# An own tile of 64 positions for batches 0 and 1 in the v half of a gMLP, and a new order of the program

## The chip, the cores and the metric

The kernel runs on one core of one Trainium2 chip. Its metric is the device time of one execution in microseconds (us). Of the kernel before there are three timed runs, 505.13, 502.82 and 502.2 us (median 502.82), and one profiled execution, from which all views are taken.

## The reference

There are 8 batches, 8 heads, 576 positions and 64 channels per head, so 512 model channels. The gMLP has 1024 hidden channels: 512 for u and 512 for v.

```python
# attention without a score matrix
q_s = exp(q - max(q, axis=-1));  q_s = q_s / sum(q_s, axis=-1)     # over the 64 channels
k_s = exp(k - max(k, axis=2));   k_s = k_s / sum(k_s, axis=2)      # over the 576 positions
kv  = einsum('bhsd,bhse->bhde', k_s, v)                            # 64 x 64 for each head
x   = einsum('bhsd,bhde->bhse', q_s, kv)                           # heads side by side: (8, 576, 512)
# gMLP
h    = gelu_tanh(x @ w_in)                                         # (8, 576, 1024)
u, v = h[..., :512], h[..., 512:]
v_n  = (v - mean(v)) / sqrt(var(v) + 1e-6) * g_ln                  # over the 512 channels of v
v_s  = einsum('ts,bsd->btd', w_sg, v_n) + b_sg                     # mixes the positions
out  = x + (u * v_s) @ w_out
```

Everything is float32.

## The kernel before

**Arithmetic.** A float32 operand is split into a high and a low part, both of type fp32r, and each large product is made of three matmul groups: high x high, low x high, high x low. So x is kept as `x_h` and `x_l`, v_n as `vnh` and `vnl`, the gated product as `gh` and `ulow`, the weights as `wi_h` and `wi_l` (w_in), `ws_h` and `ws_l` (w_sg), `wo_h` and `wo_l` (w_out). Making the low part of a product that stands in PSUM is a subtraction on DVE (VectorE); in some places TensorE adds minus the high part to the PSUM tile (steps named ..._neg, matmuls with `minus`), and ACT (ScalarE) then only copies.

**Steps of one batch.** q is loaded, reduced by its maximum over the channels (`q_max`, `q_sub`, `q_exp`, `q_sum`, `q_inv`, `q_mul`) and transposed. k is reduced by its maximum over the positions (`k_ma` to `k_maxb`, `k_sub`, `k_exp`), and `kv_mm` gives kv, which `kv_scale` divides by the sum of k. `x_mm` (batch 1), `xf_mm` (batch 0, in parts) or `xm_mm` (batches 2 to 7) give x transposed, channels on partitions; the steps ..._high and ..._low write `x_h` and `x_l`. `hu_mm` and `hu_part` give u, again transposed, in four pieces of 128 channels. `hv_mm` gives v with positions on partitions, tile by tile of 128 positions: x is the stationary operand, `wi_h` and `wi_l` are moved in 512 columns, 12 matmuls a tile. Per tile follow the gelu (`hv_gelu`, ACT), the statistics (`hv_stat`: bn_stats on DVE, or sums that ACT made in `hv_gelu` and `hv_sq`), `hv_pow` (POOL, that is GpSimd), `hv_norm` (DVE), `hv_high` (ACT) and `hv_low` (DVE). `sg_mm` is the product with w_sg, four pieces a batch, each with 24 matmuls over the four whole tiles and then the tail; `gate`, `gate_high` and `gate_low` follow, then `out_mm`, `out_base` (x back from its parts), `out_add` and `out_store`. The last piece of the last batch is done in two halves of the positions: `last_mm`, `last_add`, `last_store`.

**576 positions in tiles of 128.** Four tiles leave a tail of 64. The kernel before stores odd batches with the tail in front, and copies an odd batch's tail a second time, behind the 576 positions of the even batch before it. One v tile of 128 rows, `hv_mm b 4` with b even, then holds the tails of both batches (`tail`, L791; `tail_high`, `tail_low` and `tail_again` make its parts of v_n for either batch). So the v half of batch 0 is complete only when x of batch 1 stands. The second copies are the second pair in `x_places` (L720, batch 1) and `tail_places` (L703, later odd batches).

**What sets the order.** `PLAN` (L33) is a text of 1243 steps. It is run from first to last, and every engine gets its instructions in that order; nothing is reordered later. A letter at a step's end names the engine (V is DVE, A is ACT, G is POOL), where there is a choice. All instructions of DVE, ACT, POOL and of SP (the DMA queue) go through one helper (L156 in the profile), all matmuls through another (L243). PSUM has three double banks (`ps2`) and two single ones (`ps1`) which are taken in turn, so a step that writes a bank waits until the last reader of the step before it in that bank is done. Two slots each of `x_h`, `x_l`, q, k and kv are shared by the batches in turn; pieces of w_out wait in the second slots of `x_h` and `x_l` (the names `raw_x_h`, `raw_x_l`), until they are converted (`wo_a` to `wo_l`) and x of batch 1 may be written. Pieces of w_in are converted by `wi_a` to `wi_l`; `wi_x` lets TensorE do a part of it (matmuls with `ot_i,eye` and `wi_h,minus`).

## Time and profile before

| | us |
|---|---|
| three timed runs | 505.13, 502.82, 502.2 |
| profiled execution | 502.31 |
| its span | 500.2 |
| TensorE busy in the span | 484.3 |
| DVE, ACT, POOL busy | 359.8, 273.8, 149.5 |
| first product with w_in on TensorE | starts at 30.83 |
| first sg matmul of batch 0 | starts at 77.98 |

The span is the time from the first to the last instruction that the profile holds; the profiled execution's own time is 2.1 us longer. The granted clock of TensorE was 1.0. In a row of the timeline stand the start, the length, the engine, line and operation, the output and the inputs, the shapes and the number of instructions in a row of the same kind; in brackets the idle time before it and who ended it. In a row of groups stand the number of instructions, then busy time and mean in ns of one, then the idle time ahead of them and its releaser.

### The profile page before, as it was taken

What the parts mean: (1) busy time and instruction counts of PE and PEld (TensorE: products, weight loads), DVE (VectorE), ACT (ScalarE), POOL (GpSimd) and SP (SyncE); (2) the same over time, 40 slices, a digit from 0 to 9 for tenths busy, and PEclk for the clock granted to TensorE, in tenths of its full rate; (3) what the DMA queues carried; (4) which work ended last, traced back from release to release, by engine and by line L of the source; (5) the groups of instructions that cost most, each with busy time, mean ns of one, the idle gap of its engine ahead of it and who ended that gap; (6) DMA issues with size and microseconds to landing.
All of it is one profiled execution on the core that took longest, in us unless ns stands there. A gap on an engine that the chain in (4) does not pass through costs nothing.

```text
span 500.2 us, 9413 instructions
## 1 busy us (share of the span) xinstructions
PE 484.3 (97%) x3833; PEld 445.5 (89%) x3833; DVE 359.8 (72%) x634; ACT 273.8 (55%) x573; POOL 149.5 (30%) x122
## 2 busy tenths in 40 slices
...
GB/s 300 365 388 170 54 307 1 7 232 149 18 1 96 255 54 29 25 215 136 1 47 3 193 85 72 0 78 160 171 2 1 1 96 1 1 24 72 1 0 96
DMA packets 19630, 48.87 MB, mean 98 GB/s; under 512 B 1666, under 2 KB 8196, under 8 KB 19588
## 3 DMA queue, kind: packets, MB, share of 16 engines
...
q14 instruction: 12, 0.10, 0.1%
...
## 4 chain that ended last, share of the span: by engine, by line
PE 83%; DVE 10%; ACT 4%; issue 2%; DMA 1%; POOL 0%; ACTq 0%; POOLq 0%
PE ps L243 83%; DVE o L156 1%; DVE qd L156 1%; DVE km L156 1%; DVE qq L156 1%; DVE qm L156 1%; DVE v L156 1%; ACT qq L156 1%; DVE qt L156 1%; ACT L156 1%; DVE vnl L156 1%; DMA qq<-q_flat 1%; DVE ulow L156 0%; ACT u L156 0%; ACT wi_h L156 0%
## 5 line engine op out<-in xcount | busy, mean ns | idle before, releaser
L156 POOL TENSOR_TENSOR rs<-ve,half 128x1 f32<-128x1 f32 x36 | 27.1, 760 | 119.1 <-DVE ve L156 119.1
L156 DVE TENSOR_TENSOR u<-ps,u 128x576 f32<-128x576 f32 x32 | 24.0, 753 | 50.3 <-PE ps L243 45.6
L243 PE MATMUL ps<-gh,wo_h 128*128 128x288 f32 x256 | 56.2, 298 | 0.5 <-DVE o L156 0.5
L156 POOL TENSOR_TENSOR ulow<-u,gh 128x576 fp32r<-128x576 f32 x19 | 27.5, 1445 | 94.9 <-ACT gh L156 68.4
L243 PE MATMUL ps<-ulow,wo_h 128*128 128x288 f32 x256 | 55.5, 296 | 0.0
L243 PE MATMUL ps<-gh,wo_l 128*128 128x288 f32 x256 | 55.4, 295 | 0.0
L243 PE MATMUL ps<-ws_h,vnl 128*128 128x288 f32 x256 | 55.1, 296 | 0.2 <-DVE vnl L156 0.2
L243 PE MATMUL ps<-ws_h,vnh 128*128 128x288 f32 x256 | 55.1, 296 | 0.0
L243 PE MATMUL ps<-ws_l,vnh 128*128 128x288 f32 x256 | 54.9, 296 | 0.0
L156 ACT CAST gh<-u 128x576 fp32r<-128x576 f32 x32 | 21.2, 671 | 56.8 <-DVE u L156 56.8
L156 ACT ACT_TABLE_LOAD x30 | 38.5, 1283 | 8.3 <-DMA qq<-q_flat 3.5
L243 PEld LDWEIGHTS ps<-ws_h,vnh 128*128 128x128 f32 x256 | 41.8, 188 | 1.0
L243 PEld LDWEIGHTS ps<-gh,wo_h 128*128 128x128 f32 x256 | 41.2, 188 | 1.4 <-DVE o L156 0.8
L243 PE MATMUL ps<-x_h,wi_h 128*128 128x288 f32 (+2 forms) x256 | 40.6, 298 | 1.5 <-DVE qm L156 1.5
L243 PEld LDWEIGHTS ps<-ws_h,vnl 128*128 128x128 f32 x256 | 41.3, 188 | 0.5 <-DVE vnl L156 0.4
L243 PEld LDWEIGHTS ps<-ulow,wo_h 128*128 128x128 f32 x256 | 41.2, 188 | 0.1
L243 PEld LDWEIGHTS ps<-ws_l,vnh 128*128 128x128 f32 x256 | 41.3, 188 | 0.0
L243 PEld LDWEIGHTS ps<-gh,wo_l 128*128 128x128 f32 x256 | 41.2, 188 | 0.0
L243 PE MATMUL ps<-wi_h,x_h 128*128 128x512 f32 x144 | 40.2, 400 | 0.4 <-ACT v L156 0.3
L156 DVE TENSOR_TENSOR o<-ps,o 128x576 f32<-128x576 f32 (+1 forms) x33 | 24.1, 733 | 22.9 <-PE ps L243 20.7
L156 ACT ACTIVATE vnh<-v,rs 128x512 fp32r<-128x512 f32 x32 | 22.9, 719 | 32.0 <-DVE v L156 22.2
L243 PE MATMUL ps<-x_h,wi_l 128*128 128x288 f32 (+2 forms) x256 | 40.0, 296 | 0.0
...
## 6 DMA issues: line engine op xcount, KB each, us to landing
...
```

The costliest lines, as they stand in the source:

```text
L156: ins = op(*args, **kw)
L243: tc.keep_in_program_order(nc.tensor.matmul(*args, **kw))
```

## The change

Batches 0 and 1 (`ALONE`) no longer share a v tile. Both have the natural order of positions, and each has a fifth v tile of 64 rows, `hv_mm 0 4` and `hv_mm 1 4`, with the steps behind it on 64 rows. Batch 1's tail is no longer copied behind batch 0's positions. The other six batches share tiles as before. The transposes of batch 0's q, which is stored in tiles of 128 rows, now always take whole tiles, the last of them too. `PLAN` is written anew from first to last, 1260 steps, with other choices of engines: 24 of 37 v tiles, in place of 15 of 36, have their sums made by ACT, and 13 in place of 21 use bn_stats; POOL makes 4 in place of 2 of the subtractions `k_sub`, 17 in place of 13 of `out_base` and 10 in place of 19 of `gate_low`. The helper lines of the kernel after are L163 (DVE, ACT, POOL, SP) and L250 (TensorE).

DVE, around the x_l of batch 0 that is read out of PSUM ahead of the first product with w_in (`x_l` is that low part; `qm` the maximum of q and `km` that of k; `ot_i` is a piece of w_in or w_out in conversion, `kvt` the kv product). Before:

```order
L156 TENSOR_TENSOR kvt_1_288<-ps_1_79,kr_1_281 128x128
L156 TENSOR_TENSOR kvt_0_294<-ps_0_78,kr_0_258 128x128
L156 SCALAR_TENSOR_TENSOR ot_i_205<-raw_vnh,ot_i_205 128x512 x2
L156 TENSOR_SCALAR ot_i_305<-ot_i_305 128x512
L156 SCALAR_TENSOR_TENSOR ot_i_305<-raw_wo_h,ot_i_305 128x512
L156 TENSOR_REDUCE qm_1_328<-qq_1_296 128x36
L156 TENSOR_TENSOR x_l_335<-ps_0_75,x_h_307 128x2x256
L156 TENSOR_SCALAR ot_i_326<-ot_i_326 128x512
L156 TENSOR_TENSOR x_l_335<-ps_1_76,x_h_307 128x2x320
```

and now:

```order
L163 TENSOR_TENSOR km_0_317<-kk_0_260 128x512
L163 TENSOR_SCALAR kr_1_320<-ps_1_79 128x2
L163 RECIPROCAL kr_1_320<-kr_1_320 128x2
L163 TENSOR_TENSOR kvt_1_323<-ps_1_79,kr_1_320 128x128
L163 TENSOR_TENSOR x_l_325<-ps_1_76,x_h_278 128x2x256
L163 SCALAR_TENSOR_TENSOR ot_i_184<-raw_vnh,ot_i_184 128x512
L163 TENSOR_TENSOR km_0_317<-km_0_317 128x256
L163 TENSOR_TENSOR km_0_317<-km_0_317,kk_0_260 128x256
L163 TENSOR_SCALAR ot_i_314<-ot_i_314 128x512
L163 TENSOR_TENSOR x_l_325<-ps_2_77,x_h_278 128x2x320
```

The maximum of batch 1's q has left the place ahead of these two x_l, and steps of the maximum of batch 1's k stand there.

TensorE, at the end of batch 1's x product (`qt` is q transposed; the v tiles are the groups of three rows with `wi_h` and `wi_l`; `x_h_307` and, now, `x_h_278` belong to batch 0, `x_h_672` and `x_h_734` to batch 1). Before:

```order
L243 MATMUL ps_2_77<-qt_1_590,kvt_1_702 64x288 x2
L243 MATMUL ps_0_75<-qt_1_590,kvt_1_702 64x288 x2
L243 MATMUL ps_2_77<-qt_1_590,kvt_1_702 64x288 x2
L243 MATMUL ps_0_75<-qt_1_590,kvt_1_702 64x288 x2
L243 MATMUL ps_1_76<-x_h_672,minus 128x288 x2
L243 MATMUL ps_1_79<-wi_h,x_h_307 128x512 x4
L243 MATMUL ps_1_79<-wi_h,x_l_335 128x512 x4
L243 MATMUL ps_1_79<-wi_l,x_h_307 128x512 x4
L243 MATMUL ps_0_78<-wi_h,x_h_672 128x512 x4
L243 MATMUL ps_0_78<-wi_h,x_l_704 128x512 x4
L243 MATMUL ps_0_78<-wi_l,x_h_672 128x512 x4
```

and now:

```order
L250 MATMUL ps_0_78<-wi_h,x_h_278 64x512 x4
L250 MATMUL ps_0_78<-wi_h,x_l_325 64x512 x4
L250 MATMUL ps_0_78<-wi_l,x_h_278 64x512 x4
L250 MATMUL ps_0_75<-qt_1_683,kvt_1_679 64x288 x2
L250 MATMUL ps_1_76<-qt_1_683,kvt_1_679 64x288 x2
L250 MATMUL ps_0_75<-qt_1_683,kvt_1_679 64x288 x2
L250 MATMUL ps_1_76<-qt_1_683,kvt_1_679 64x288 x2
L250 MATMUL ps_1_79<-wi_h,x_h_734 128x512 x4
L250 MATMUL ps_1_79<-wi_h,x_l_765 128x512 x4
L250 MATMUL ps_1_79<-wi_l,x_h_734 128x512 x4
```

The tail tile (128 rows for two batches before, 64 rows for batch 0 now) has moved from behind batch 1's x product to ahead of its second half, and a whole tile of batch 1 now follows that product directly. The subtraction of x_h by TensorE has gone.

TensorE, ahead of sg of batch 1 (the rows with `ws_h`; the rows of 288 columns with `wi_h` and `wi_l` are a piece of u). Before:

```order
L243 MATMUL ps_1_76<-qt_0_1335,kvt_0_1462 64x512 x4
L243 MATMUL ps_0_78<-qt_0_1335,kvt_0_1462 64x64 x2
L243 MATMUL ps_1_79<-qt_0_1335,kvt_0_1462 64x64 x2
L243 MATMUL ps_2_77<-qt_1_1420,kvt_1_1323 64x512 x4
L243 MATMUL ps_0_78<-qt_1_1420,kvt_1_1323 64x64 x2
L243 MATMUL ps_1_79<-qt_1_1420,kvt_1_1323 64x64 x2
L243 MATMUL ps_0_75<-ws_h,vnh 128x288 x2
```

and now:

```order
L250 MATMUL ps_0_75<-x_h_734,wi_h 128x288 x8
L250 MATMUL ps_0_75<-x_h_734,wi_l 128x288 x8
L250 MATMUL ps_0_75<-x_l_765,wi_h 128x288 x8
L250 MATMUL ps_1_79<-wi_h,x_h_734 64x512 x4
L250 MATMUL ps_1_79<-wi_h,x_l_765 64x512 x4
L250 MATMUL ps_1_79<-wi_l,x_h_734 64x512 x4
L250 MATMUL ps_0_78<-wi_h,x_h_1438 128x512 x4
L250 MATMUL ps_0_78<-wi_h,x_l_1470 128x512 x4
L250 MATMUL ps_0_78<-wi_l,x_h_1438 128x512 x4
L250 MATMUL ps_1_76<-ws_h,vnh 128x288 x2
```

The new tile of batch 1 stands there, between a piece of u and the first v tile of batch 2 (`x_h_1438`), and that tile is followed by sg of batch 1.

The diff, cut to its core. Of `PLAN` only the last lines are shown.

```diff
+ALONE = [0, 1]
+def second(b):
+
+    return 0 if b in ALONE else b % 2
...
-out_mm 7 0, out_base 7 0 V, out_base 7 3 V, out_add 7 0, out_store 7 0, out_mm 7 1, out_add 7 1, out_store 7 1, out_mm 7 2, out_add 7 2, out_store 7 2
-last_mm 7 0, last_add 7 0, last_store 7 0, last_mm 7 1, last_add 7 1, last_store 7 1
+gate_high 7 3, gate_low 7 3 V, out_mm 7 1, out_add 7 1, out_store 7 1, out_base 7 0 G, out_mm 7 0, out_add 7 0, out_store 7 0, out_base 7 2 G
+out_base 7 3 V, last_mm 7 0, last_add 7 0, out_mm 7 2, out_add 7 2, out_store 7 2, last_mm 7 1, last_store 7 0, last_add 7 1, last_store 7 1
...
     def qtr_mm(b, h, s):
         ps = bank(ps2, "qt", b, h, s)
         for z in range(2):
             for m, i in enumerate(range(TILES[s].start, TILES[s].stop)):
-                n = TL if i == ST else P
-                from_ = flat_q(b, h)[0:n, i, 2 * z:2 * z + 2].rearrange("p g d -> p (g d)")
-                mm(ps[:, z, m * P:m * P + n], from_, eye[0:n, 0:n], is_transpose=True, start=True, stop=True)
+                from_ = flat_q(b, h)[:, i, 2 * z:2 * z + 2].rearrange("p g d -> p (g d)")
+                mm(ps[:, z, m * P:m * P + P], from_, eye, is_transpose=True, start=True, stop=True)
...
     def main_tail(b):
-        o = b % 2 * TL
+        o = second(b) * TL
...
     def whole(x, b):
-        return x(b, at=b, shape=[P, NP, S + TL * (1 - b % 2)])
+        return x(b, at=b, shape=[P, NP, S + TL * (b not in ALONE and not second(b))])
...
     def x_places(x, b, p):
-        yield ps2_of(b, p)[:, :, 0:HS], split(x(b, at=b, shape=[P, NP, S + TL * (1 - b % 2)])[:, p, 0:S])
-        if b % 2:
+        yield ps2_of(b, p)[:, :, 0:HS], split(whole(x, b)[:, p, 0:S])
+        if second(b):
             yield ps2_of(b, p)[:, 0, 0:TL], x(b - 1)[:, p, S:S + TL]
...
+    def rows(b, i):
+        return slice(0, TL if i == ST and b in ALONE else P)
+
     def hv_mm(b, i):
-        col = ST * P if i == ST else (b % 2) * TL + i * P
+        col, n = ST * P if i == ST else second(b) * TL + i * P, rows(b, i)
...
-            mm(ph, lhs(b)[:, c, col:col + P], rhs[:, c, DV:2 * DV], start=m == 0, stop=m == len(pairs) - 1)
+            mm(ph[n], lhs(b)[:, c, col:col + n.stop], rhs[:, c, DV:2 * DV], start=m == 0, stop=m == len(pairs) - 1)
...
     def hv_gelu(b, i, E=V):
+        n = rows(b, i)
...
-            A.activation(v_s(b, i), st["hv", b, i], AF.Gelu_apprx_tanh, accum_out=sm_s(b, i))
+            A.activation(v_s(b, i)[n], st["hv", b, i][n], AF.Gelu_apprx_tanh, accum_out=sm_s(b, i)[n])
...
     def tail(b):
 
-        e, i = b - b % 2, b % 2
+        i = second(b)
+        e = b - i
...
     def sg_mm(b, d):
-        o, ds = TL - (b % 2) * TL, slice(d * P, (d + 1) * P)
+        o, ds = TL - second(b) * TL, slice(d * P, (d + 1) * P)
...
-    qo = np.stack([q[b][:, order[b % 2]] for b in range(B)])
+    qo = np.stack([q[b][:, order[second(b)]] for b in range(B)])
...
-        res[b, order[b % 2][:, None], chan] = got[b].T
+        res[b, order[second(b)][:, None], chan] = got[b].T
```

`hv_sq`, `hv_stat`, `hv_pow` and `hv_norm` take the same `rows` as `hv_gelu`; `tail_places` (the tails of later batches) asks `second(b)` in place of `b % 2`, as `x_places` does.

More of the change, by code (lines that the diff above doesn't have):

```diff
@@ L52 @@
-q_mul 1 0 1 G, q_turn 1 1, hv_mm 0 3, k_exp 1 1, hv_gelu 0 3 A, hu_part 0 3 0, hu_gpart 0 3 0, wo_b 2, wo_c 3, wo_z 0, wo_b 0 A, x_mm 1 0, ws_h 0
-ws_l 0 G, wo_d 0, wo_h 0, wo_c 2, wo_d 2, x_high 1 0, x_high 1 1, ws_h 1, wo_d 3, kv_mm 1 1, kv_inv 1 1, kv_scale 1 1, x_low 1 0, q_turn 1 3
-hv_stat 0 1, hv_pow 0 1, load_g, hv_norm 0 1, hv_sq 0 3, hv_stat 0 3 A, hv_mm 0 2, hv_gelu 0 2 A, load_k 2 1, k_ma 2 1, x_mm 1 1, x_high 1 2
-x_low 1 2, x_high 1 3, x_low 1 3, load_q 2 1, hv_stat 0 0 A, x_neg 1 1, x_low 1 1 A, hv_norm 0 0, hv_sq 0 2, hv_stat 0 2 A, hv_norm 0 2, wo_h 2
@@ new lines @@
+load_w_sg 0, xf_mm 0 1 1, xf_high 0 1 1, xf_mm 0 1 0, xf_high 0 1 0, wi_l 2 G, ws_h 0, wi_d 0, wi_x 3, xf_neg 0 1 0, k_mb 1 0, k_mc 1 0, wi_b 5
+xf_neg 0 1 1, xf_low 0 0 1, wi_c 5, wi_h 0, q_max 1 1, xf_low 0 1 0 A, kt_mm 1 0, xf_low 0 1 1 A, load_w_in 7, wi_a 7, k_top 1 0, wi_l 0 G, load_k 1 1
+k_ma 1 1, load_q 1 0, hu_part 0 1 0, hu_gpart 0 1 0, wi_d 5, wi_h 5, hu_part 0 0 1, wi_b 7, wi_l 3 A, load_w_in 6, q_swapm 1 1, hu_gpart 0 0 1
+k_mb 1 1, hu_part 0 2 0, hu_gpart 0 2 0, wi_c 7, wi_a 6, kb_mm 1 0, load_w_in 4, q_max 1 0, wi_a 4, wi_d 7, hu_part 0 3 0, q_swapm 1 0, load_w_out 0
@@ new lines @@
+load_v 1 0, hu_part 0 0 0, q_top 1 1, k_mc 1 1, kt_mm 1 1, k_sub 1 0 V, hu_part 0 2 1, hu_gpart 0 0 0, k_top 1 1, wi_h 7, hu_gpart 0 3 0, kb_mm 1 1
+q_top 1 0, load_w_sg 2, wi_b 6, wi_c 6, hu_part 0 3 1, wi_b 4, wi_d 6, wi_c 4, k_exp 1 0, wi_l 5 G, wi_l 7 V, wi_d 4, k_sub 1 1 V, wi_h 6, q_sub 1 1 G
+q_exp 1 1, wi_h 4, load_w_out 1, wo_a 1, kv_mm 1 0, kv_inv 1 0, kv_scale 1 0, k_exp 1 1, hu_part 0 1 1, q_sum 1 1, wi_l 4 V, wi_l 6 G, hv_mm 0 3
+hv_mm 0 0, load_w_out 3, wo_a 3, ws_l 0 V, q_sub 1 0 G, q_exp 1 0, wo_b 3, wo_c 3, load_w_out 2, wo_b 1, q_swapd 1 1, q_inv 1 1, q_mul 1 1 1 G
@@ L659, in xf_places @@
     def xf_places(x, b, h, s):
-        return st["x", b, h, s][:, :, 0:width(s)], x(b, at=b, shape=[P, NP, S + TL])[:, 2 * h:2 * h + 2, COLS[s]]
+        return st["x", b, h, s][:, :, 0:width(s)], whole(x, b)[:, 2 * h:2 * h + 2, COLS[s]]
     def xf_high(b, h, s):
```

222 lines of the change are left out of this document (111 added, 111 removed).

## The prediction

> **What bounds the kernel now.** I read the page's busy shares first, then the busy time of each engine in stretches, cut where the TensorE (PE) row changes: 30.8 is the first product with w_in, 78.0 the first spatial product (sg) of batch 0, 124 the end of that batch's output. In a stretch's row stand start and end, its length, then busy time and instructions of PE, PEld, DVE (VectorE), ACT (ScalarE) and POOL (GpSimd), the granted clock, the DMA share and GB/s.
>
> ```profile
> PE 484.3 (97%) x3833; PEld 445.5 (89%) x3833; DVE 359.8 (72%) x634; ACT 273.8 (55%) x573; POOL 149.5 (30%) x122
> ```
> ```profile
> 30.80:78.00 47.20, 46.74 (x330) 38.06 (x331) 45.06 (x85) 45.17 (x97) 21.60 (x15) 1.00 0.53 198
> 78.00:124.00 46.00, 45.37 (x417) 43.92 (x415) 43.51 (x78) 29.23 (x70) 15.77 (x11) 1.00 0.31 97
> 124.00:410.00 286.00, 286.00 (x2321) 265.77 (x2311) 213.98 (x371) 157.63 (x338) 77.38 (x58) 1.00 0.22 77
> 410.00:494.50 84.50, 84.34 (x596) 81.67 (x594) 31.55 (x53) 19.71 (x34) 17.91 (x16) 1.00 0.06 22
> ```
>
> From 124 to 494.5 PE idles 0.16 of 370.5 us: there an edit counts only by the matmuls it adds or removes. In 30.8 to 78 three engines are full at once: PE 46.74, DVE 45.06 and ACT 45.17 of 47.20. So time can come only from the start up to 78, from the small gaps in 78 to 124, and from the last microseconds. Next, the waits of PE and (up to 66 us) of DVE: total, times, longest.
>
> ```profile
> PE ps L243 <- DVE qm L156: 1.5, 1, 1.5
> PE ps L243 <- DVE kvt L156: 0.9, 2, 0.6
> PE ps L243 <- DVE o L156: 0.5, 1, 0.5
> ```
> ```profile
> DVE qm L156 <- DMA qq<-q_flat: 3.5, 1, 3.5
> DVE kr L156 <- PE ps L243: 1.7, 3, 0.8
> DVE qd L156 <- ACT qq L156: 0.5, 1, 0.5
> DVE x_l L156 <- ACT x_h L156: 0.4, 1, 0.4
> DVE ot_o L156 <- ACT ot_o L156: 0.4, 1, 0.4
> DVE ot_i L156 <- ACT ot_i L156: 0.4, 1, 0.4
> ```
>
> Past the first load (3.5 us) DVE waits only 1.7 + 0.5 + 3 x 0.4 = 3.4 us in 66. Its queue sets the pace up to sg of batch 0. Last, the rows in order of time: PE at the first product, at the hv tiles ahead of batch 0's sg, and one row of the kv product; then DVE's last x_l of batch 1 and ACT's high part of batch 0's tail.
>
> ```profile
> 30.83 0.83 PE L243 MATMUL ps<-x_h,wi_h 128*128 128x320 f32 x4 [1.49 <-DVE qm L156]
> ...
> 34.08 1.02 PE L243 MATMUL ps<-ot_i,eye 128*128 128x512 f32 x2
> ...
> 35.17 0.64 PE L243 MATMUL ps<-x_h,wi_h 128*128 128x256 f32 x4
> ```
> ```profile
> 62.74 0.54 PE L243 MATMUL ps<-x_h,minus 128*128 128x288 f32 x2
> 63.12 1.02 PE L243 MATMUL ps<-wi_h,x_h 128*128 128x512 f32 x3
> 64.31 0.50 PE L243 MATMUL ps<-wi_h,x_h 128*128 128x512 f32 x1 [0.16 <-ACT x_h L156]
> ...
> 66.78 1.10 PE L243 MATMUL ps<-wi_h,x_h 128*128 128x512 f32 x4
> ...
> 69.58 1.10 PE L243 MATMUL ps<-wi_h,x_h 128*128 128x512 f32 x4
> ...
> 72.38 1.10 PE L243 MATMUL ps<-wi_h,x_h 128*128 128x512 f32 x4
> ...
> 77.98 0.43 PE L243 MATMUL ps<-ws_h,vnh 128*128 128x288 f32 x2
> 78.25 0.43 PE L243 MATMUL ps<-ws_h,vnl 128*128 128x288 f32 x2
> ...
> 96.20 2.55 PE L243 MATMUL ps<-vv,kk 128*64 128x65 f32 x80
> ```
> ```profile
> 63.78 1.67 DVE L156 TENSOR_TENSOR x_l<-ps,x_h 128x576 fp32r<-128x576 f32 x4
> ```
> ```profile
> 73.03 0.71 ACT L156 ACTIVATE vn<-v,rs 64x512 fp32r<-64x512 f32 x1
> ```
>
> DVE's last x_l of batch 1 ends at 63.78 + 1.67 = 65.45. One undisturbed hv tile takes 72.38 - 69.58 = 2.80 us (12 matmuls, 0.233 each). The tail tile took 66.78 - 63.12 = 3.66, that is 0.86 too long: it read batch 1's tail, whose x_h and x_l came in just then.
>
> **The change part by part.** I sum against the profiled execution, 502.31 us (span 500.2, and 2.1 around it); it lies 0.5 below the median, within the runs' spread.
>
> (a) *The new tile, hv 1 4.* Twelve matmuls with 512 columns, half as many rows as a full tile. No row shows such a shape. Above: the 3.66 of the stretched tail tile. Below: 12 x 2.55/80 = 0.4 us (the group at 96.20, 80 matmuls of a far smaller shape), if the cost went by output area. I take 2.80: a tile of as many columns. It stands in the part where PE never idles, so it counts in full. Batch 0's own tail tile replaces the shared one at the same price: 0.
>
> (b) *Work that goes from the start.* Four ACT and four x_l copies of batch 1's tail go, and one of three wi_x steps (35.17 - 34.08 = 1.09 us of PE) and one x_neg (63.12 - 62.74 = 0.38); an xf_neg of that size comes. Four transposes of q grow from 64 to 128 columns; PE waits around them in the start, so nothing. All this shortens PE's list from the first product to sg 0, which is not what ends it (rival A).
>
> (c) *The place of sg 0.* DVE's list up to the last x_l of batch 1, by group means, is 64.30 us (110 instructions) before and 64.91 (109) now. The rows that differ most:
>
> ```profile
> L156 DVE TENSOR_TENSOR x_l<-ps,x_h 128x64 fp32r<-128x64 f32 x3 | 0.6, 213 | 0.0
> L156 DVE TENSOR_TENSOR qq<-qq,qd 128x768 f32<-128x768 f32 x1 | 1.0, 951 | 0.0
> L156 DVE TENSOR_TENSOR qq<-qq,qd 128x512 f32<-128x512 f32 x1 | 0.7, 683 | 0.0
> L156 DVE TENSOR_TENSOR qq<-qq,qd 128x576 f32<-128x576 f32 x12 | 10.2, 862 | 0.2
> L156 DVE BATCH_NORM_STATS2 s<-v 128x6 f32<-128x512 f32 x21 | 14.3, 681 | 2.8 <-ACT v L156 2.8
> L156 DVE SCALAR_TENSOR_TENSOR v<-v,nm,g_bc 128x512 f32<-128x512 f32 x15 | 12.2, 815 | 0.0
> L156 DVE SCALAR_TENSOR_TENSOR vnl<-v,rs,vnh 128x512 fp32r<-128x512 f32 x32 | 25.7, 819 | 9.2 <-ACT vnh L156 9.2
> L156 DVE TENSOR_TENSOR ws_l<-ghws,ws_h 128x640 fp32r<-128x640 f32 x2 | 1.6, 822 | 0.0
> ```
>
> Out go three tail copies (0.64), two qf_mul (0.951 + 0.683) and one bn_stats (0.681); in come a q_mul (0.862), a net norm (0.815), a low part of v_n (0.819) and a w_sg low part (0.822); small steps make the rest, net +0.61. Against that stand DVE's waits of 3.4 us: the early part of the order is written anew, and the tail tile no longer waits for batch 1. If all go, the last x_l ends at 65.45 + 0.61 - 3.4 = 62.7; if none, 66.1. I take 2.0 of them, a little over half, as no row decides: 64.1. In the new order hv 1 3 follows batch 1's x product directly, so PE waits for that x_l: of hv 1 3 eight matmuls still need it (1.87), then three tiles (8.40), then sg 0: 64.1 + 10.3 = 74.4 against 77.98. Lead 3.6 us (5.0 if all waits go, 1.6 if none). What is late next is ACT: its list up to the tail's high part is, by the same kind of sum, 2.9 us longer, so that part would end at 73.74 + 2.9 = 76.6. sg needs it only behind its 24 matmuls on the whole tiles, 12 x (78.25 - 77.98) = 3.2 us after its start, at 77.6: covered by a microsecond.
>
> (d) *POOL against DVE.*
>
> ```profile
> 87.78 3.33 POOL L156 TENSOR_TENSOR kk<-kk,km 128x1280 f32<-128x1280 f32 x1
> ```
> ```profile
> 90.12 1.60 DVE L156 TENSOR_TENSOR o<-x_h,x_l 128x576 f32<-128x576 f32 x1
> ...
> 112.70 0.75 DVE L156 TENSOR_TENSOR o<-x_h,x_l 128x576 f32<-128x576 f32 x1
> ```
>
> The same DVE step takes 1.60 us where it starts under a POOL subtraction (which ends at 91.11; the step ends 0.61 later), and 0.75 alone. POOL's steps ahead of sg 0 grow by 1.4 us by their rows. I price that at 0: DVE loses time only where two steps meet, and both orders have such meetings. Upper end +1.4, if each added POOL microsecond stops DVE for one. The Trainium skill, page "SBUF — State Buffer", section "Who interferes with whom", says that VectorE and GpSimd share a port pair under an exclusive lock, so that the later one stands still for the other's whole instruction; the two rows agree, and by that rule the sum would lie at most that upper end higher. Behind 124, POOL also takes two k_sub of 3.7 us from DVE:
>
> ```profile
> L156 POOL TENSOR_TENSOR kk<-kk,km 128x1280 f32<-128x1280 f32 x2 | 7.4, 3699 | 8.8 <-issue 8.7
> ```
>
> They stand far ahead of their kv products; DVE idles 286.00 - 213.98 = 72 us there: 0, or some 2 us each if the cover were gone (rival C).
>
> (e) *hv 1 4's own chain.* It stands on PE ahead of hv 2 1, and sg of batch 1 needs its tail behind the same 24 matmuls. Cover: 2.80 + 3.2 = 6.0. DVE's three steps (0.681 + 0.815 + 0.819 = 2.3) and about as much on ACT and POOL make some 5 us: 0, or up to 1 us late if DVE is busy with another step.
>
> (f) *The end and 78 to 124.* out_mm 7 2 now lies between the two last halves, so last_mm 7 1 needn't wait for `o` : -0.5 (0 if the wait moves elsewhere). Of the waits on kvt (0.9) I let 0.6 go, the longer one, as batch 2's kv now stands in another place; ends 0 and 0.9.
>
> Sum: 502.31 - 3.6 (c) + 2.80 (a) - 0.6 - 0.5 (f) = 500.4; forecast **500.5 us**.
>
> **The rivals.** *A, PE's own list is the limit:* DVE's waits go and the x_l comes early. DVE's list up to the x_l ahead of the first product is 1.87 us shorter (the two qf_mul and a q max leave it, three k max steps come), and some 2.0 of the 3.4 us of waits lie ahead of it: first product at 30.83 - 3.9 = 27.0. PE's list from there to sg 0 was 47.15, less its idle time (47.20 - 46.74 = 0.46) and the stretch of 0.86, that is 45.8, and loses 1.09: 44.7. sg 0 at 71.7, lead 6.3: 502.31 + 2.8 - 6.3 - 0.9 - 0.5 = 497.4 (496 with the tail chains fully covered and a cheaper tile, 498.6 where only part comes). For it: DVE's queue in the first 31 us is the one that got shorter. Against it: DVE has as much to do by hv 1 3 as before. Chance 0.18.
>
> *B, no lead at all, hence slower:* at hv 1 3 PE now waits for the x_l with no other tile between, where before the tail tile and three others stood behind it. If DVE's queue isn't drained sooner (its waits turn up elsewhere, or POOL stops it for the 1.4 of (d)), sg 0 starts at 76.4 to 77.8, a lead of 1.6 to 0.2, and hv 1 4 is paid in full: 502.31 + 2.8 - 1.6 = 503.5, up to 504.9. It decides from a last x_l later than 64.9 (sg 0 at 75.2, where the lead equals the tile's 2.80). Chance 0.20.
>
> *C, new waits behind 124:* the order of batches 2 to 7 is new too, and PE has 0.16 us of idle there, so any of the many chains can only get worse. One microsecond at each of six sg's gives 500.4 + 6 = 506.4. Against it: DVE idles 72 us and ACT 128 of 286 there. Chance 0.10.
>
> That the change doesn't do what it says is no rival: 24 new matmuls of 64 rows (12 in place of the shared tile's) stand in the order.
>
> **How the numbers follow.** Forecast 0.52 (498.6 to 503.5, from the bounds of (c), (e) and (f)), A 0.18, B 0.20, C 0.10. The predicted time is the forecast's. The range of 8 in 10 leaves out C's upper part and the edge of A: 496.0 to 504.5. About 1% (5 us, 497.8 to 507.8) is what a measurement of this kernel can tell from no change. Faster than that: most of A and a little of the forecast's lower edge, 0.22. Slower: the upper half of C with a bad B, 0.06. Within: 0.72.
>
> **What would show it.** (a) the 24 rows of 64x512 at about 0.233 us each; half of that would make the tile 1.4. (c) the last x_l of batch 1 at 64.1 and sg 0 at 74.4: at 71.7 it is A, from 75.2 on B; and a PE wait for x_l in hv 1 3. DVE's waits up to there of about 1.4 us in place of 3.4. (d) DVE rows of twice their mean under POOL's. (f) no wait for `o` in the last 10 us. PE idle from sg 0's output to the end still under 0.5 us; several microseconds would be C. The prediction is wrong if the time leaves 498.6 to 503.5, and its reasons are if the time fits with sg 0 where it was.

## The result

The kernel after takes 498.75 us (median of 6 runs, 498.42 to 499.33), the kernel before 502.69 us beside it. The ratio is 0.991 (95% interval 0.988 to 0.994); in a second set of runs, on one of the three chips of the experiments, it was 0.993 (0.990 to 0.996). That is 0.7 to 0.9% faster, inside the 1% that the prediction called no change, and 1.75 us under the predicted 500.5. It lies only 0.15 above 498.6, the lower end of the band that the prediction gave its likeliest case, and the profiled execution (498.42) lies just below that end.

The page of the profile after, its busy line, and its stretches (cut at the first product with w_in, 27.25, and at sg of batch 0, 73.18; columns as before):

```profile
PE 483.2 (97%) x3858; PEld 444.2 (89%) x3858; DVE 351.9 (71%) x617; ACT 285.6 (58%) x607; POOL 150.7 (30%) x123
```
```profile
27.25:73.20 45.95, 45.33 (x326) 36.53 (x325) 44.64 (x80) 42.48 (x98) 22.43 (x17) 1.00 0.66 227
73.20:124.00 50.80, 50.65 (x439) 47.34 (x438) 48.43 (x83) 34.41 (x81) 15.16 (x14) 1.00 0.30 100
124.00:410.00 286.00, 285.42 (x2320) 265.10 (x2319) 204.04 (x358) 167.15 (x356) 83.11 (x60) 1.00 0.22 75
```

The shape is the same: three full engines up to sg of batch 0, then a TensorE almost without gaps. DVE lost 8 us of work in all and ACT took 12; by itself that says little of the time, since behind 124 TensorE is busy in 285.42 of 286.00 us. What moved are three marks. TensorE's rows around them, of the kernel after:

```profile
27.25 0.73 PE L250 MATMUL ps<-x_h,wi_h 128*128 128x256 f32 x4
...
59.72 1.68 PE L250 MATMUL ps<-qt,kvt 64*64 64x288 f32 x16
61.32 1.40 PE L250 MATMUL ps<-wi_h,x_h 128*128 128x512 f32 x4
62.56 1.46 PE L250 MATMUL ps<-wi_h,x_l 128*128 128x512 f32 x4
63.86 1.10 PE L250 MATMUL ps<-wi_l,x_h 128*128 128x512 f32 x4
...
73.18 0.43 PE L250 MATMUL ps<-ws_h,vnh 128*128 128x288 f32 x2
...
76.69 0.80 PE L250 MATMUL ps<-ws,vn 128*128 128x288 f32 x4
...
119.01 1.09 PE L250 MATMUL ps<-wi_h,x_h 128*64 128x512 f32 x4
...
121.81 1.09 PE L250 MATMUL ps<-wi_h,x_h 128*128 128x512 f32 x4
```

| stretch of TensorE | before | after | difference |
|---|---|---|---|
| start to the first product with w_in | 30.83 | 27.25 | -3.58 |
| first product to sg of batch 0 | 47.15 | 45.93 | -1.22 |
| sg of batch 0 to the end of the span | 422.22 | 423.32 | +1.10 |
| span | 500.2 | 496.5 | -3.7 |

The last line but one holds the new tile (121.81 - 119.01 = 2.80) and what went against it: the wait on kvt (0.63) and the wait for the add at the end (0.71, with the restart) are gone. Another 0.36 that went are a balance of small gains and losses; among the losses are new waits of some 0.3 us (ahead of 76.69) and 1.0 us (at 228 to 231). By these marks the earlier first product (3.58) is as large as nearly the whole gain (3.7); behind it, 1.22 us gained ahead of sg of batch 0 and 1.10 lost behind it almost cancel.

**Why the first product is earlier.** The start of the kernel before and after, TensorE's rows (small matmuls on the identity; `eye,qq` and `eye,x_lk` are transposes, `vv,kk` the kv product). Before:

```profile
13.47 4.70 PE L243 MATMUL ps<-eye,x_lk 128*128 128x128 f32 x19 [0.19 <-ACT x_lk L156]
17.97 2.99 PE L243 MATMUL ps<-eye,qq 128*128 128x128 f32 x12
20.89 2.55 PE L243 MATMUL ps<-vv,kk 128*64 128x65 f32 x80
```

After:

```profile
6.51 4.37 PE L250 MATMUL ps<-eye 128*128 128x128 f32 x20 [6.51 <-DMA eye<-identity]
10.72 0.60 PE L250 MATMUL ps<-eye,qq 128*128 128x128 f32 x4
11.15 1.25 PE L250 MATMUL ps<-eye,x_lk 128*128 128x128 f32 x10
```

Before, twelve transposes at 18 us still take 0.24 us each (20.89 - 17.97 over 12). After, those from 10.7 us on take 0.11 (11.15 - 10.72 over 4), half of it. The views print a clock of 1.00 in both starts; the trace's own clock records begin with the first grant of the full clock, at 19.74 us before and at 10.47 us after. So in the start the rate is read from the pace of equal rows. The 31 transposes quoted of before cost TensorE some 4 us more than at the pace of after (31 x 0.13, an estimate); how much of that reaches the first product is another matter, taken up below.

The new order runs seven `warm` steps, 14 matmuls on the identity whose output nothing reads, ten of them back to back as soon as the identity has landed; the order before ran three such steps, with waits for q and k between them and the transposes. The Trainium skill, page "TensorE: Matmul & The Clock Gate", section "What's actually happening", says that TensorE starts at half rate and is let to full rate after some 3.4 us of sustained activity. The rows of after agree: 4.2 us of back to back matmuls stand ahead of the full rate (6.51 to 10.72). Those of before agree less well: from 13.47 to the grant at 19.74 the transposes run for 6.3 us, with one listed gap of 0.19 us ahead of them, and still at half rate.

Before, DVE and ACT waited for TensorE in the start, and those waits nearly went. DVE's and ACT's waits for it in the first 33 us before, and ACT's after (DVE has none left there):

```profile
DVE kr L156 <- PE ps L243: 1.1, 2, 0.8
...
ACT qt L156 <- PE ps L243: 1.7, 3, 0.9
```
```profile
ACT qt L163 <- PE ps L250: 0.3, 1, 0.3
```

How much of the 3.58 us is the rate's? The experiment e12 (below) has the old order of the lists and a TensorE that got the full clock at 17.13 us, and in its start DVE no longer waits for TensorE at all. Its first product still comes at 29.64. So against the execution of before the rate is worth some 1.2 us (30.83 - 29.64), about the 1.1 us that DVE had waited for TensorE; the other 2.4 (29.64 - 27.25) come with the new order. The kv product of batch 0 says the same. Its last row in the kernel after, then in e12:

```profile
20.40 1.39 PE L250 MATMUL ps<-vv,kk 128*64 128x65 f32 x40
```
```profile
19.03 2.65 PE L250 MATMUL ps<-vv,kk 128*64 128x65 f32 x80
```

It ends at 21.8 after, at 21.7 in e12 and at 23.4 before. From there to the first product it is 5.5 us after, but 8.0 in e12 and 7.4 before. Directly ahead of the first product, TensorE waited for DVE for 1.49 us before (the row is in the prediction) and 1.48 in e12; after, that wait is gone. The first product stands behind an x_l of DVE, so here are all engines' busy times up to the end of that x_l, before and after (columns as in the stretches):

```profile
0.00:30.68 30.68, 19.96 (x172) 14.42 (x172) 24.64 (x47) 21.91 (x39) 16.84 (x22) 1.00 0.98 340
```
```profile
0.00:26.72 26.72, 18.07 (x188) 13.99 (x189) 21.54 (x46) 20.15 (x34) 16.02 (x21) 1.00 0.97 343
```

DVE has 3.1 us less to do up to there (24.64 to 21.54) and idles 0.9 less (6.04 to 5.18). So the larger part of the lead is DVE's shorter list, and the faster rate is the smaller. e1 (below), which puts one q maximum back on that list, moves the first product by 2.2 us, 1.0 of it a wait for a load.

That the `warm` steps bring the full rate was read from the traces and not tried by taking them away, and e12 and the kernel before are compared here by one execution each. So the split of the 3.58 us is an estimate.

### The profile page after: what moved, and what is told of

The parts are those of the page before. It is cut to its first block, busy times and chain, and to the rows that moved or that the text cites. A ratio compares the mean times of both kernels' runs of the same rounds, so it can differ in the third digit from the quotient of the medians.

```text
span 496.5 us, 9491 instructions
## 1 busy us (share of the span) xinstructions
PE 483.2 (97%) x3858; PEld 444.2 (89%) x3858; DVE 351.9 (71%) x617; ACT 285.6 (58%) x607; POOL 150.7 (30%) x123
## 4 chain that ended last, share of the span: by engine, by line
PE 82%; DVE 7%; ACT 6%; DMA 2%; issue 1%; POOL 0%; SPq 0%; ACTq 0%
PE ps L250 82%; DMA raw_wo_h<-w_in 2%; DVE km L163 1%; DVE x_l L163 1%; DVE vnl L163 1%; DVE ot_o L163 1%; ACT qq L163 1%; ACT ot_i L163 1%; ACT L163 1%; DVE qm L163 1%; ACT kk L163 1%; DMA qq<-q_flat 1%; DVE v L163 1%; ACT u L163 1%; DVE qt L163 0%
## 5 line engine op out<-in xcount | busy, mean ns | idle before, releaser
L250 PE MATMUL ps<-gh,wo_h 128*128 128x288 f32 x256 | 55.8, 296 | 0.0
L250 PE MATMUL ps<-ulow,wo_h 128*128 128x288 f32 x256 | 55.3, 295 | 0.0
L250 PE MATMUL ps<-gh,wo_l 128*128 128x288 f32 x256 | 55.3, 295 | 0.0
L250 PE MATMUL ps<-ws_h,vnh 128*128 128x288 f32 x256 | 55.0, 296 | 0.0
L250 PE MATMUL ps<-ws_h,vnl 128*128 128x288 f32 x256 | 54.9, 296 | 0.0
L250 PE MATMUL ps<-ws_l,vnh 128*128 128x288 f32 x256 | 54.8, 295 | 0.0
L163 POOL TENSOR_TENSOR rs<-ve,half 128x1 f32<-128x1 f32 (+1 forms) x37 | 27.2, 743 | 78.8 <-DVE ve L163 68.4
L163 POOL TENSOR_TENSOR qq<-qq,qd 128x576 f32<-128x576 f32 (+2 forms) x20 | 27.4, 1384 | 67.4 <-DVE qd L163 60.6
L163 DVE TENSOR_TENSOR u<-ps,u 128x576 f32<-128x576 f32 x32 | 23.8, 751 | 32.1 <-PE ps L250 32.1
L163 ACT CAST gh<-u 128x576 fp32r<-128x576 f32 x32 | 20.9, 670 | 43.4 <-DVE u L163 43.2
L250 PEld LDWEIGHTS ps<-ws_h,vnh 128*128 128x128 f32 x256 | 41.6, 188 | 0.7
L163 DVE TENSOR_TENSOR o<-ps,o 128x576 f32<-128x576 f32 (+1 forms) x33 | 23.9, 728 | 25.3 <-PE ps L250 22.8
L250 PEld LDWEIGHTS ps<-gh,wo_h 128*128 128x128 f32 x256 | 41.3, 188 | 0.6
L250 PE MATMUL ps<-wi_h,x_l 128*128 128x512 f32 (+1 forms) x148 | 41.0, 397 | 0.6 <-DVE x_l L163 0.4
L250 PEld LDWEIGHTS ps<-ws_h,vnl 128*128 128x128 f32 x256 | 41.3, 188 | 0.1
L250 PEld LDWEIGHTS ps<-gh,wo_l 128*128 128x128 f32 x256 | 41.3, 188 | 0.0
L250 PEld LDWEIGHTS ps<-ws_l,vnh 128*128 128x128 f32 x256 | 41.3, 188 | 0.0
L250 PEld LDWEIGHTS ps<-ulow,wo_h 128*128 128x128 f32 x256 | 41.1, 188 | 0.0
L163 DVE SCALAR_TENSOR_TENSOR vnl<-v,rs,vnh 128x512 fp32r<-128x512 f32 x32 | 27.1, 860 | 19.8 <-ACT vnh L163 19.7
L250 PE MATMUL ps<-wi_h,x_h 128*128 128x512 f32 (+1 forms) x148 | 40.9, 397 | 0.1
L250 PE MATMUL ps<-x_h,wi_h 128*128 128x288 f32 (+2 forms) x256 | 40.8, 299 | 0.0
```

The costliest lines, as they stand in the source:

```text
L163: ins = op(*args, **kw)
L250: tc.keep_in_program_order(nc.tensor.matmul(*args, **kw))
```

## The experiments

Two theories stood against each other for the stretch up to sg of batch 0. D, the forecast's: DVE's list to the last x_l of batch 1 sets it. P, rival A's: TensorE's own list does, from the first product on. In the edits, `PLAN` steps are shown as lines.

**e1: one DVE step put back ahead of the first product.**

```diff
+q_max 1 1,
 xf_low 0 0 0, ..., xf_low 0 0 1, wi_c 5, wi_h 0,
-q_max 1 1,
 xf_low 0 1 0 A, ...
```

> The kernel after with one DVE step put back: the maximum of batch 1's q (1.35 us) stands again ahead of the two x_l of batch 0 that come before the first product with w_in. DVE's list up to the last x_l of batch 1 is as long as before the edit. Theory D (DVE's list up to that x_l sets sg of batch 0, as forecast): the first product starts up to 1.3 us later than 27.25, PE's wait at batch 1's x product shrinks by as much, the last x_l still ends at 63.5 and sg 0 starts at 73.2 to 73.4; time within 0.3 us of 498.75. Theory P (TensorE's own list, from the first product on, sets it): sg 0 starts as much later as the first product, up to 74.5, and the time is up to 1.3 us longer.

Measured 502.13 us, ratio 1.000 (0.998 to 1.002); first product at 29.44, sg 0 at 75.09. The step had also to wait for its load (DVE's waits in the run):

```profile
DVE qm L163 <- DMA qq<-q: 1.0, 1, 1.0
```

So the delay was 2.2 us in place of 1.3, and it came through to sg 0 nearly in full: 75.09 - 29.44 = 45.65, against 45.93. This leans to P, no more: the wait for the load makes DVE's list longer too, by 1.0 us, and the last x_l of batch 1 came at 65.36, 1.90 us later, where D had it stay at 63.5. The times add a doubt. The profiled execution is the shortest of the ten, 500.47 us. Six of the ten took 502.07 to 502.86 us at a mean granted clock of 0.996 to 0.997, which would be 3 to 4 us at half clock (0.0035 x 500 / 0.5, an estimate); no trace shows where in the kernel.

**e2: DVE relieved between batch 1's x_l.**

```diff
-hv_low 0 3, x_low 1 1, hv_norm 0 0, ..., x_low 1 3,
+x_low 1 1, ..., x_low 1 3, hv_low 0 3, hv_norm 0 0,
-q_max 2 1, q_swapm 2 1, tail_low 0
+tail_low 0, q_max 2 1, q_swapm 2 1
```

> The kernel after with two DVE steps of 0.66 us each (the low part of v_n of tile 3 and the norm of tile 0 of batch 0), which stand between the x_l of batch 1, put behind the last of them, and the maximum of batch 2's q (1.33 us) put behind batch 0's tail, so that the tail isn't late instead. Theory D: the last x_l of batch 1 ends up to 1.3 us earlier than 63.46, sg 0 starts at 72.2 to 72.6 in place of 73.18 (TensorE's own list allows 72.1), and the time falls by 0.6 to 1.0 us. Theory P: sg 0 and the time stay where they are, within 0.2 us.

Measured 500.47 us, ratio 0.998 (0.997 to 0.999): slower than the kernel after. DVE's x_l and TensorE's wait among the tiles in this run:

```profile
61.73 1.42 DVE L163 TENSOR_TENSOR x_l<-ps,x_h 128x576 fp32r<-128x576 f32 x2 [0.85 <-ACT x_h L163]
```
```profile
68.48 1.20 PE L250 MATMUL ps<-wi_h,x_h 128*128 128x512 f32 x4 [0.79 <-ACT v L163]
```

Both theories miss. The last x_l ended only 0.3 us earlier, since its high part on ACT hangs on TensorE's x product; and the low part put behind it was late in freeing the buffer of v that the next gelu writes, which held up ACT, and then TensorE, by 0.8 us. sg 0 came at 74.18.

**e3 and e6: the tile of batch 0 put behind batch 1's x product, without and with a filler in its place.**

```diff
 # e3
-hv_mm 0 4, ..., x_mm 1 1, ..., hv_mm 1 3, hv_gelu 1 3 A,
+x_mm 1 1, ..., hv_mm 1 3, hv_mm 0 4, hv_gelu 1 3 A, hv_gelu 0 4 A,
 # e6: besides
-x_mm 1 1,
+fill 6, x_mm 1 1,
+    def fill(n):
+        for z in range(2):
+            ps = bank(ps1, "fill", n, z)
+            for m in range(n):
+                mm(ps, x_h(0)[:, 0, 0:P], wi_h[:, 0, DV:2 * DV], start=m == 0, stop=m == n - 1)
```

> The kernel after with the 64-row tile of batch 0 put behind the first v tile of batch 1, where the kernel before has its tail tile: behind batch 1's x product. Theory D: that product can't come earlier, since its bank waits for a DVE step at 60.15, so TensorE idles where the tile stood, the last x_l still ends near 63.5, and behind it stand one tile more: sg 0 at 75.5 to 76.0, the time 2.3 to 2.8 us longer, about 501.3. Theory P: the order of TensorE's list among the v tiles is free; the x product comes 2.8 us earlier and sg 0 stays at 73.2, the time at 498.8.

> The order of experiment e3 (batch 0's 64-row tile behind batch 1's x product and first v tile), and in the tile's old place, ahead of that product, twelve matmuls of the same shape as a v tile's whose output nothing reads: added work. Theory C (in e3 the 2.7 us in which TensorE had nothing to do cost twice, because its granted clock fell to 0.50 until 66 us): with the gap filled the clock stays at 1.00, the x_l and the tiles behind run as in the kernel after, and one tile more stands behind them: sg 0 at 75.5 to 76.2 in place of 78.66, so twelve useless matmuls make the kernel some 2.5 us faster than e3. Rival W (e3 lost the time to its waits on DVE and ACT, the clock is a bystander): sg 0 stays at 78 to 79, as TensorE arrives no earlier at the x product.

e3: 503.14 us, ratio 1.002 (1.001 to 1.004), sg 0 at 78.66. e6: 501.32 us, ratio 0.998 (0.996 to 1.000), sg 0 at 76.60. First e3's stretches (TensorE's busy time, the others', and the granted clock, third from the end) and its x product; then the same of e6:

```profile
58.00:60.00 2.00, 0.00 (x0) 0.00 (x0) 2.00 (x6) 2.00 (x5) 1.96 (x2) 0.98 0.00 0
60.00:62.00 2.00, 1.91 (x14) 1.21 (x16) 2.00 (x5) 0.54 (x2) 2.00 (x3) 0.50 0.40 129
62.00:64.00 2.00, 2.00 (x9) 0.97 (x4) 1.67 (x3) 1.65 (x4) 0.26 (x1) 0.50 1.00 408
64.00:66.00 2.00, 2.00 (x7) 1.52 (x6) 1.97 (x4) 1.38 (x4) 0.00 (x0) 0.50 0.94 367
66.00:68.00 2.00, 2.00 (x9) 1.48 (x8) 2.00 (x5) 1.43 (x3) 1.06 (x2) 0.82 0.07 28
```
```profile
60.09 2.83 PE L250 MATMUL ps<-qt,kvt 64*64 64x288 f32 x16 [2.66 <-DVE qt L163]
```
```profile
60.00:62.00 2.00, 2.00 (x20) 0.85 (x18) 2.00 (x4) 0.99 (x3) 2.00 (x3) 1.00 0.32 78
62.00:64.00 2.00, 2.00 (x9) 1.14 (x7) 2.00 (x4) 1.78 (x5) 0.40 (x1) 1.00 1.01 406
```
```profile
57.47 3.05 PE L251 MATMUL ps<-wi_h,x_h 128*128 128x512 f32 x12
60.45 1.60 PE L251 MATMUL ps<-qt,kvt 64*64 64x288 f32 x16
```

In e3 TensorE waits 2.66 us for a DVE transpose of q, as D said, and then runs at half clock until about 66.7 us, 6.6 us after it went on (0.82 in the last row shown is 0.7 us of 0.50). In e6 the gap is filled with twelve matmuls that compute nothing, the clock stays at 1.00, and sg 0 comes 2.06 us earlier, if 0.4 later than C's band. So the useless work makes the kernel 1.8 us faster than e3 (C had 2.5), and W, by which the clock was a bystander and sg 0 would have stayed at 78 to 79, is out. The two ran on different chips, but e3's own eight executions, all on one chip, say the same: 503.07 to 503.82 us where the mean granted clock was 0.992 or 0.993, 502.08 at 0.995, 501.75 at 0.997 and 501.08 at 1.000. Against the kernel after, e6 is one tile later (76.60 - 27.91 = 48.69 from its first product, against 45.93: 2.76). That does not tell D from P, as e6's TensorE list is longer by the same twelve matmuls. That a tile ahead of the x product is free there is shown by e3: without it TensorE idles for 2.66 us.

**e4: the new order without the split.**

```diff
-ALONE = [0, 1]
+ALONE = []
-hv_mm 0 4, ..., x_mm 1 1, ..., hv_mm 1 3,
+x_mm 1 1, ..., hv_mm 1 3, hv_mm 0 4,
+hv_norm 0 4, tail_high 1, tail_low 1,
-hv_mm 1 4, hv_gelu 1 4, hv_stat 1 4, hv_norm 1 4, hv_pow 1 4, tail_high 1, tail_low 1
```

> The new order without the split: batches 0 and 1 share one tail tile of 128 rows again (batch 1's tail in front and copied behind batch 0's positions, four copies more on ACT and DVE), which stands behind the first v tile of batch 1; batch 1's own 64-row tile and its steps are left out of the order. Theory D: DVE's list is 4 x 0.21 = 0.85 us longer to the last x_l, and one tile more stands behind it: sg 0 at 76.5 to 77, that is 3.5 later, and 2.80 come back where batch 1's tile stood: 0.5 to 1.0 us slower than the kernel after, 499.3 to 499.8. So the split itself would be worth under 1 us, and the rest is the order's. Theory P: sg 0 stays near 73.5 and the 2.80 are saved: 496.2. A third theory, that the split made the whole gain: the time goes back to about 502.

Measured 503.88 us, ratio 1.007 (1.004 to 1.010): the third theory's size, against both D and P.

```profile
59.66 2.30 PE L250 MATMUL ps<-qt,kvt 64*64 64x288 f32 x16 [2.67 <-DVE qt L163]
...
82.41 0.80 PE L250 MATMUL ps<-ws,vn 128*128 128x288 f32 x4 [1.69 <-DVE vn L163]
```

A shared tile needs batch 1's x and so can't stand ahead of its product. The same gap opens as in e3, 2.67 us. The clock falls to 0.50 again, but for half as long, from about 61.1 to 64.6 us (0.79, 0.50 and 0.86 in the stretches of 2 us from 60 on). sg 0 comes at 77.18, and the shared tile's own chain is then 1.7 us late. Part of the 5 us lies in the place where I put the tile's steps; that the gap opens does not.

**e12: the split without the new order.** The kernel after's functions, the kernel before's `PLAN`, with batch 1's tile put in:

```diff
+hv_mm 1 4, hv_gelu 1 4,
 hv_mm 2 1, hv_gelu 2 1,
+hv_stat 1 4, hv_norm 1 4, hv_pow 1 4, tail_high 1, tail_again 1, tail_low 1, sg_mm 1 2, out_base 1 1 V
```

> The split alone: the kernel before with an own 64-row tile for batches 0 and 1, in the order of before; batch 1's tile and the steps behind it are put in ahead of batch 2's first v tile, nothing else moves. Here TensorE had no gap ahead of batch 1's x product that a tile could fill: sg 0 gains the 0.86 us by which the shared tile was stretched (77.1 in place of 78.0), and the new tile costs 2.80: 1.9 us slower than before, ratio 1.004. If the split itself brought the lead, sg 0 would start 3 us or more earlier and the time would be that of before or less.

Measured 506.38 us, ratio 1.007 (1.005 to 1.010): slower by 3.7 us by the ratio (4.2 between the medians) rather than 1.9. First product and sg 0 are 47.06 us apart (47.15 before), 0.09 less and not the 0.86 expected, so the split alone brings no lead. Behind it, the new tile has a wait of its own:

```profile
124.49 1.14 PE L250 MATMUL ps<-wi_h,x_h 128*64 128x512 f32 x4 [1.46 <-DVE x_l L163]
```

2.80 for the tile, 1.46 for this wait; the rest is not assigned. As placed in e4 and here, split and order are worth something only together.

**e9 and e10: each engine held back by itself.**

```diff
 # e9
+fill 10, hu_part 0 1 0        (20 matmuls eye x eye into two single banks)
 # e10
+spend, spend, x_low 1 0       (bn_stats of 512 columns of wi_h, written to a tile that nothing reads)
```

> The kernel after with twenty small matmuls on the identity (128x128, about 0.07 us each, 1.4 us together; nothing reads them) ahead of the first product with w_in: TensorE's own list is 1.4 us longer to sg of batch 0, DVE's and ACT's are not. Theory D (DVE's list to the last x_l of batch 1 sets sg 0): TensorE's wait of 1.1 us at that x_l takes most of it up, sg 0 moves by 0.3 us. Theory P (TensorE's list sets it): sg 0 and the time move by 1.4 us.

> The kernel after with two DVE statistics steps whose output nothing reads (0.68 us each, 1.36 together) ahead of the first x_l of batch 1: DVE's list is 1.36 us longer to the last x_l, TensorE's is not. Theory D: the last x_l ends at 64.8, sg 0 starts at 74.5 and the time is 1.3 us longer. Theory P: sg 0 stays within 0.3 us of 73.2; batch 0's tail, which comes later by as much on DVE, may cost up to 1 us there.

In e9 the filler also writes over a PSUM bank from which a low part of one piece of w_in was still to be read, so that piece's values differ; the number and order of the other instructions do not. It took far more than I expected (fp32 matmuls on the identity stand as two records, 0.11 us each):

```profile
27.65 4.63 PE L251 MATMUL ps<-eye 128*128 128x128 f32 x40
32.04 0.72 PE L251 MATMUL ps<-x_h,wi_h 128*128 128x256 f32 x4
...
77.38 0.43 PE L251 MATMUL ps<-ws_h,vnh 128*128 128x288 f32 x2
```

e9: 503.05 us, ratio 1.001 (0.999 to 1.003). The first product is 4.79 us later than in the kernel after, sg 0 4.20 later: TensorE has 0.6 us of slack up to sg 0, no more. That DVE and ACT wait with it for its products would explain this, but was not measured. e10: 499.84 us, ratio 0.995 (0.992 to 0.997).

```profile
61.76 1.19 PE L252 MATMUL ps<-qt,kvt 64*64 64x288 f32 x12 [1.06 <-DVE x_l L164]
```

Its x product waits 1.06 us for the held x_l, the last x_l ends at 65.02 and sg 0 starts at 74.77 (D had 64.8 and 74.5). From the first product that is 47.32, against 45.93: the 1.36 us come through in full, 1.39. At the end 0.8 us of them are left against the kernel after in e5 (499.04), less than D's 1.3; that run was on another chip, where the kernel before took 502.03 us, against 502.19 here. So P is right on a late first product and D on a longer DVE list: both lie on the path.

**e5: the kernel after once more.**

> The kernel after itself, on the chip on which the three kernels beside it run, since the kernel before gave 501.85 us where the first four experiments ran and 502.69 us where the kernel after was first timed. Every theory: the ratio 0.991 again, sg of batch 0 at 73.2.

499.04 us, ratio 0.993 (0.990 to 0.996), first product at 27.65, sg 0 at 73.58: 45.93 apart again.

**e7: two waits of the kernel after mended.**

```diff
-q_max 2 1, q_swapm 2 1, tail_low 0
+tail_low 0, q_max 2 1, q_swapm 2 1
-hv_high 3 0, hv_low 3 0, k_mb 5 0, k_mc 5 0, k_fold 5 0, xm_mm 4, ..., xm_low 4 1
+xm_mm 4, ..., xm_low 4 1, hv_high 3 0, hv_low 3 0, k_mb 5 0, k_mc 5 0, k_fold 5 0
```

> The kernel after with two places mended that its trace shows: the maximum of batch 2's q (1.33 us of DVE) goes behind batch 0's tail, for which TensorE waits 0.3 us at 76.4; and the high and low part of batch 3's tile 0 with three steps of batch 5's k go behind batch 4's x_l, for which TensorE waits about 1.0 us at 228 to 231. If both waits go and nothing comes in their place: 1.0 to 1.3 us faster than the kernel after. If the next late thing stands right behind them, as in e2: 0 to 0.3.

500.41 us, ratio 0.996 (0.994 to 0.998): slower than the kernel after. Both waits went, and two others came (TensorE's waits in this run):

```profile
PE ps L250 <- ACT v L163: 1.3, 1, 1.3
...
PE ps L250 <- DVE u L163: 0.6, 1, 0.6
```

The first, at 242, is a gelu that stands on ACT behind batch 5's exp; the moved DVE steps pushed batch 5's q maximum back by 1.5 us, and with it POOL's and ACT's steps. The second, at 85, is a gate of batch 0, behind DVE steps of batch 2 that now come later. No version faster than the kernel after came out of these runs.

**e8: the kernel before with the new end.**

```diff
-out_mm 7 2, out_add 7 2, out_store 7 2, last_mm 7 0, last_add 7 0, last_store 7 0, last_mm 7 1,
+last_mm 7 0, last_add 7 0, out_mm 7 2, out_add 7 2, out_store 7 2, last_mm 7 1, last_store 7 0,
```

> The kernel before with the new order of the last steps alone: the third output piece goes between the two halves of the last one. The wait for the add (0.55, with its restart 0.71) at 494.3 to 495.1 goes: 0.5 to 0.7 us faster than before, as in the prediction's term (f). The rival that the wait moves to the second half's bank: 0.

501.44 us, ratio 0.998 (0.996 to 0.999): 0.6 us faster, as expected; the wait on `o` is gone. The interval leaves 0.4 to 2.1 us. Its profiled execution is the longest of its eleven, 503.67 us, and shows how much the old start varies. TensorE's rows in it:

```profile
18.61 3.67 PE L243 MATMUL ps<-eye,qq 128*128 128x128 f32 x12
22.21 3.52 PE L243 MATMUL ps<-vv,kk 128*64 128x65 f32 x80
...
33.13 0.83 PE L243 MATMUL ps<-x_h,wi_h 128*128 128x320 f32 x4 [1.50 <-DVE qm L156]
```

Here the transposes still run at half rate, and so does part of the kv product (80 took 3.52, before 2.55): full clock at 24.34 us by the clock records, first product at 33.13. In e12, which has the same order in its start, they run at full rate by 17.6, and the first product comes at 29.64:

```profile
17.63 1.47 PE L250 MATMUL ps<-eye,qq 128*128 128x128 f32 x12
...
29.64 0.53 PE L250 MATMUL ps<-x_h,wi_h 128*128 128x320 f32 x2 [1.48 <-DVE qm L163]
```

With the execution of before (full clock at 19.74, first product at 30.83) the order of the three is the same in both numbers.

**e11: a third of batch 1's tile.**

```diff
+        if (b, i) == (1, ST):
+            pairs = pairs[0:4]
```

> The kernel after with batch 1's 64-row tile made by its high x high group alone: 4 matmuls in place of 12 (the low parts of 64 positions are left out). It measures what a matmul of that shape is worth at the end of the kernel. Prediction's term (a), that the tile counts in full: 8 x 0.233 = 1.87 us faster than the kernel after, 496.9 to 497.1. Rival, that the tile is hidden beside other work or costs by its rows: 0 to 0.9 us.

498.68 us, ratio 0.992 (0.989 to 0.995). The kernel after gave 0.993 and 499.04 us in e5, on another chip, and 498.75 in its first runs: 0.1 to 0.4 us of the 1.87 are left. All six runs, 498.23 us the lowest, lie above the 496.9 to 497.1 that term (a) asks for. Batch 2's first v tile, directly behind, in this run:

```profile
123.20 0.73 PE L250 MATMUL ps<-wi_h,x_l 128*128 128x512 f32 x2 [0.76 <-DVE x_l L163]
```

It now waits for batch 2's x_l, 0.94 us with the restart; sg of batch 1 starts 51.04 us behind sg of batch 0, against 51.40 (e5). The rival is right: at this place the tile covers a wait, and most of its time is not its price.

The distances put side by side, by what was edited:

| | first product | sg 0 | between |
|---|---|---|---|
| before; e8; e12 (old order) | 30.83; 33.13; 29.64 | 77.98; 80.30; 76.70 | 47.15; 47.17; 47.06 |
| after; e5; e11 (new order) | 27.25; 27.65; 27.69 | 73.18; 73.58; 73.65 | 45.93; 45.93; 45.96 |
| e1, e9 (first product held) | 29.44; 32.04 | 75.09; 77.38 | 45.65; 45.34 |
| e10 (DVE held 1.36) | 27.45 | 74.77 | 47.32 |
| e2; e7 (DVE's steps moved) | 27.39; 27.83 | 74.18; 73.77 | 46.79; 45.94 |
| e3; e6; e4 (tail tile behind the x product) | 27.79; 27.91; 27.34 | 78.66; 76.60; 77.18 | 50.87; 48.69; 49.84 |

## Why the prediction was right, and where it was not

The time lay in the range and, by 0.15 us, in the band of the likeliest case, with the sign of the sum and about twice its size: predicted -3.6, +2.80, -0.6, -0.5 make -1.9; the spans show -4.8, +2.80, -0.63, -0.71 and -0.36 unassigned, -3.7. sg of batch 0 came at 73.18, nearly midway between the forecast's 74.4 and rival A's 71.7. By its steps:

- **(c) the place of sg 0** is the term that was mis-sized: 73.18 in place of 74.4, a lead of 4.80 in place of 3.6. The last x_l ended at 63.46 (64.1 forecast; 62.72 + 0.74 in the row below). And only five matmuls of the first tile stand behind it, not eight: of its four l x h matmuls only the fourth reads the block that this x_l writes. 63.46 + 5 x 0.233 + 8.40 = 73.0. The path itself, x_l, one tile, three tiles, was as drawn, and TensorE did wait at the x product's parts (61.32 to 63.86, 2.54 for eight matmuls that take 1.87 undisturbed: 0.3 of the 0.67 in the four that need x_h, 0.4 in the four that need x_l).

```profile
62.72 0.74 DVE L163 TENSOR_TENSOR x_l<-ps,x_h 128x576 fp32r<-128x576 f32 x1
```

  Up to the end of that x_l, before and after:

```profile
0.00:65.45 65.45, 54.15 (x448) 42.41 (x448) 57.50 (x112) 55.49 (x108) 32.56 (x32) 1.00 0.73 258
```
```profile
0.00:63.46 63.46, 54.24 (x473) 43.22 (x473) 57.13 (x110) 55.35 (x110) 32.72 (x33) 1.00 0.86 298
```

  DVE idled 1.6 us less (7.95 to 6.33) where the sum took 2.0, and its work fell by 0.4 where the sum had it grow by 0.61. So the x_l came 2.0 us earlier for two reasons, of which the sum held one, too large, and the other with the wrong sign.

- **The first product** was not priced in the forecast at all, and it moved by as much as the whole gain. Rival A priced it, at 27.0 against the measured 27.25, from a DVE list shorter by 1.87 (3.1 measured) and waits of 2.0 that go (0.9 measured). So the reason was A's in kind, its two sizes were off in opposite directions, and part of the closeness is luck. That TensorE runs at half rate in the start, and that `warm`, seven steps in place of three, ends it sooner, stood neither in the forecast nor in A; e12 puts it at some 1.2 us.
- **(a) the new tile** is 2.80 long, to the hundredth. That it counts in full "in the part where PE never idles" was wrong: a gap can be absent because the tile fills it (e11). In the sum this did not show, since the wait behind it was neither in the trace of before nor in mine.
- **(b)** set the shortened list of TensorE at nothing. The 1.22 us that went between the first product and sg of batch 0 are about as long as the wi_x step that went from there (1.09: before, one of three stood behind the first product; after, both stand ahead of it). No run takes this step by itself, so that it is the cause is not shown.
- **(d)** DVE rows of two and four times their mean do stand under POOL's. The kernel after, DVE and then POOL, columns as ever:

```profile
67.22 1.80 DVE L163 TENSOR_TENSOR km<-km,kk 128x256 f32<-128x256 f32 x1
```
```profile
66.95 1.79 POOL L163 TENSOR_TENSOR ws_l<-ghws,ws_h 128x640 fp32r<-128x640 f32 x1
```

  Undisturbed, that DVE step takes 0.42. It starts 0.27 us behind POOL's and ends 0.28 behind its end. The tail's low part, at 75.89, came so late that TensorE waited 0.3 us for it (the step from 76.12 to 76.69): the price at sg 0 is 0.3, not 0 and not 1.4.
- **(e)** held: no wait stands at batch 1's tail in its sg. **(f)** held, with 0.71 and 0.63.
- **The rivals.** A's time (497.4) lies 1.35 from the measured one, the forecast's 1.75. Its number for the first product was close, the distance from there to sg of batch 0 was not: 44.7 in A, 45.93 measured, since DVE's list does hold the tiles back (e10). B did not come: TensorE's wait at that place is under 0.7 us. Of C there is one case, a wait for batch 4's x_l, about 1.0 us with its restarts at 228 to 231, which the old order did not have.
